# First eight gate/up steps beside the exponentials, their silu made later from DRAM, in a fused S4 and SwiGLU forward and backward kernel

## The chip, the cores and the metric

The kernel runs on one core of a Trainium2 chip. The metric is device microseconds of one execution. Before the change the median of three executions is 1864.86 us (1864.12 to 1871.07); one further execution was taken with the hardware profiler, and its trace is what the views below show.

## The reference, cut to what matters

Tokens L = 2048, channels D = 576, state N = 128, hidden width F = 4608, all in bfloat16. The kernel returns the output and the gradients of all inputs that count, 13 arrays in all.

```python
xn = layernorm(A_u)                                   # [2048, 576]
dt = exp(log_dt)                                      # [576]
K  = Re sum_n C * exp(dt * (A_re + i A_im) * l) * dt * B   # [576, 2048], l = 0..2047
s  = irfft(rfft(xn, 4096) * rfft(K, 4096))[:2048] + xn * Dskip
gate, up = xn @ w1, xn @ w3                           # [2048, 4608] each
g  = silu((silu(gate) * up) @ w2)
out = A_u + s * g
# and the vjp: gradients of A_u, A_re, A_im, B_re, B_im, C_re, C_im, log_dt, Dskip, w1, w3, w2 for grad_out
```

## The kernel before, in words

The program is written on a layer that orders instructions itself: every instruction carries a priority, a time in us set by `pre` (prologue, L145) or `at` (all later stages, L123), and each engine's instruction list is filled by priority as the data dependences allow. On each engine the list is then fixed when the program is built. Three things hold an instruction back beyond its data: `tc.issue_after(x)` puts it behind x; a `Chain` (L62) puts every operation behind the one before it on the same engine; and a generator that yields due times lets one stage weave its steps into another's.

Tokens lie in 16 tiles of 128, channels in five blocks of 128 (the last holds 64). The program's PSUM tiles are of one bank (512 fp32 columns on each partition) or of two, shared out by pools.

**Prologue** (`prologue`, L264 to 372). It loads log_dt, A, B and C (`load_dvec`, `load_dmat`, `load_rates`) and A_u (`ln_load`); A_u's odd token tiles are also kept with their rows turned, in DRAM (`odd_A_u`), and read back from there. It multiplies A_re by dt, splits the product into three bf16 parts (`split3`, L374), stores them (PCS_dram) and loads them back as `lhs_r` with 48 rows. `build_reader` makes SELR, a matrix of selectors. `early_exps` (L498) then forms the real exponents as 108 products of 48 rows by 512 columns, two to a PSUM buffer of two banks (`e_ps`, two buffers), 54 exponentials of 1024 columns by ScalarE (L514), and stores the factors to E_dram. Meanwhile VectorE takes the layer norm's statistics (`ln_stats`; the root by ScalarE's Sqrt), normalises (`ln_normalise`), and TensorE transposes xn to `xnT` (two two-bank buffers `ln_pt`; the 64 channels of the last block are copied to the other half of the partitions by a DMA). GpSimd multiplies C by B (the W products) and builds the selectors SEL. `early_spectra` (L519) makes the DFT of xn, folded by its symmetries, into UH_dram: 32 groups of four products of 288 columns into two two-bank buffers, each copied out by VectorE in one operation of 576 columns.

**Hidden phase** (`ffn_hidden`, L859 to 925). Nine blocks of 512 hidden columns by eight pairs of token tiles make 72 gate/up steps. A step has for each of its two tiles eight products of 512 columns of full depth (L901) and two tail products of depth 64 (L909), into `pg` and `pu` (one bank each, two buffers each). Then ScalarE makes silu into `s_t` (L913), g is copied out by VectorE for the second tile of the pair (L915) and by ScalarE for the first (L917), u by ScalarE (L918). VectorE multiplies h = s * u (L920); SP's queue stores H (L922), GpSimd's queue stores G and U (L924), which the backward pass reads.

**Woven into it** (`ssm_forward`, L469, a generator that `ffn_hidden` draws on by due times): first `ssm_kernel` (L542), 36 chunks of 16 channels that build K from the stored exponentials (load of `E_l` L570, phase products `et_ps` L589, sines `cs_k` by ScalarE L590, products on VectorE L595 to 611, sums over n as 64 matmuls into `kps` L626, copy to `KT` L630); then `ssm_conv` (L788), the convolution in two halves of the channels: DFT of K (`kraw`, L726 to 729), complex products by VectorE (`cmul_acc`, L771), inverse DFT (L761), the sums `ev` and `s_t` (L843 to 846), S to DRAM (L847). Before its chunks `ssm_forward` issues four things for the convolution on SP's queue: the row of Dskip, a turned copy of grad_out's odd tiles (`odd_grad_out`), the DFT matrices to CS_dram and four transposing loads of them (`cT`, `nat_transpose`). By priority all of these land in the prologue's part of the lists.

**Then** the output projection (`ffn_output`, L927, product `po` L976), and the backward pass (from L1034): the convolution's gradients, the parameters' gradients, and three large weight and input gradients.

The call that joins these: the pools of the hidden phase are opened after the prologue's are closed, and `ffn_hidden(wp, gup, fps, 0, 12, ssm_forward(0, 8, 8))` gives steps 6 us apart and chunks and convolution steps 8 us apart in the planner's time.

## Time and profile before

| what | value |
|---|---|
| median of three runs | 1864.86 us |
| profiled execution, time | 1858.3 us |
| its span, first to last instruction | 1856.5 us |
| mean clock granted to TensorE | 0.965 |
| TensorE matmul busy | 1679.0 us, 90% of the span |
| VectorE, ScalarE, GpSimd busy | 1370.5, 909.5 and 354.7 us |
| first product of the exponentials, last exponential done | 35.1 and 122.7 us |
| first gate product | 123.3 us |
| first sine of the chunks, last product of the chunks | 149.3 and 430.1 us |
| last inverse DFT of the convolution | 596.9 us |
| last gate product, first output projection | 598.5 and 598.7 us |

The profile cuts the span in 40 slices of 46 us, with a digit for each engine's busy tenths and one for the clock that TensorE was granted (9 is 90% or more). Its groups give, for a line of the program and an engine, the number of instructions, their busy time and the mean of one. The timeline lists single groups by start. In a table of stretches each engine has its busy time with the number of its instructions in brackets; PEld is TensorE's loading of weights, which lies beside its products. Times count from the span's start.

### The profile page before, as it was taken

The numbers are of one execution on the slowest core, as the hardware profiler recorded it, in microseconds if no ns is written. First come the engines' busy times: TensorE is split into PE (matmuls) and PEld (weight loads), VectorE is DVE, ScalarE is ACT, GpSimd is POOL, SyncE is SP. The second block draws the span as 40 slices with busy tenths as digits, with TensorE's granted clock in tenths as the row PEclk, the third lists the DMA queues.
The fourth block names the chain that finished last, engine by engine and source line by source line (L and its number), as shares of the span: only waits on it lengthen the run. The fifth ranks groups of instructions, "written<-read, shape, count | busy, mean of one in ns | idle before, by whom it ended". The sixth has DMA issues, their size and how long they took to land. (4 is left out here: it accounts for less than half of the span.)

```text
span 1856.5 us, 38320 instructions
## 1 busy us (share of the span) xinstructions
PE 1679.0 (90%) x15461; PEld 1228.5 (66%) x15516; DVE 1370.5 (74%) x2081; ACT 909.5 (49%) x1636; POOL 354.7 (19%) x569
## 2 busy tenths in 40 slices
PE   2899999999897899789999999999999987998997
PEld 0335555555353677678878888888878865786776
DVE  5648766768988455589694888849999954976684
ACT  3768888887563111476665756655544410000101
POOL 4022222222222211011111111111111143131032
PEclk9769999999998999999999999999999998999999
DMA  6579988887777988758666575579999999989994
GB/s 174 189 245 321 334 301 308 307 291 272 229 249 212 240 192 187 231 159 221 178 196 201 164 215 165 173 208 270 254 263 236 203 231 228 233 206 205 202 224 73
DMA packets 627111, 417.13 MB, mean 225 GB/s; under 512 B 425205, under 2 KB 567477, under 8 KB 622325
## 3 DMA queue, kind: packets, MB, share of 16 engines
q1 hardware_dynamic: 568644, 280.65, 60.3%
q0 software_dynamic: 31728, 107.69, 17.2%
q10 hardware_dynamic: 26560, 26.35, 5.0%
q8 instruction: 121, 1.98, 0.4%
q14 instruction: 58, 0.47, 0.1%
HBM read 135.60 MB, written 190.89 MB: 176 GB/s over the span
## 5 line engine op out<-in xcount | busy, mean ns | idle before, releaser
L1672 PEld LDWEIGHTS <-acts 128*128 128x128 bf16 x2304 | 225.8, 99 | 78.2 <-DMA acts<-GG_dram 9.4
L1624 PEld LDWEIGHTS <-xn_bf 128*128 128x128 bf16 x2304 | 224.7, 98 | 34.8 <-issue 8.7
L1241 DVE TENSOR_TENSOR pr_q<-et_ps,pz 128x1024 f32<-128x1024 f32 x144 | 176.0, 1222 | 32.3 <-PE et_ps L1236 24.6
L1672 PE MATMUL px<-wT,acts 128*128 128x288 bf16 x1408 | 181.1, 288 | 4.3 <-DMA wT<-in_B_w_dram 4.3
L901 PEld LDWEIGHTS <-xnT 128*128 128x128 bf16 x1152 | 107.4, 98 | 115.5 <-issue 25.5
L1564 PE MATMUL ph<-w2T,goT 128*128 128x256 bf16 x1440 | 175.3, 277 | 8.6 <-DMA w2T<-w2r 6.8
L1244 DVE TENSOR_REDUCE S_all<-pr_q 128x32 f32<-128x1024 f32 x144 | 175.3, 1217 | 3.3
L901 PE MATMUL pg<-wmB_w,xnT 128*128 128x512 bf16 x526 | 148.1, 383 | 16.1 <-DVE g_t L915 9.5
L1564 PEld LDWEIGHTS <-goT 128*128 128x128 bf16 x1440 | 141.3, 99 | 27.4 <-DMA w2T<-w2r 7.1
L901 PE MATMUL pu<-wmB_w,xnT 128*128 128x512 bf16 x571 | 155.7, 379 | 0.4
L1604 PE MATMUL pgw<-go_o,h_n 128*128 128x288 bf16 x1152 | 150.3, 289 | 6.3 <-DVE h_n L1542 5.5
L1624 PE MATMUL pgw<-gu_n,xn_bf 128*128 128x256 bf16 x1152 | 133.9, 274 | 6.5 <-ACT gw L1608 6.3
L1604 PEld LDWEIGHTS <-h_n 128*128 128x128 bf16 x1152 | 113.3, 99 | 35.2 <-DVE h_n L1542 5.7
L1672 PE MATMUL px<-wA,acts 128*128 128x288 bf16 x896 | 120.4, 292 | 13.8 <-DMA acts<-GG_dram 9.0
L913 ACT ACTIVATE s_t<-pg 128x512 bf16<-128x512 f32 x144 | 87.8, 610 | 89.8 <-PE pu L909 45.1
L1624 PE MATMUL pgw<-gg_n,xn_bf 128*128 128x256 bf16 x1152 | 130.0, 273 | 0.6 <-ACT gw L1626 0.6
L1567 ACT CAST gh<-ph 128x512 bf16<-128x512 f32 x144 | 82.2, 602 | 78.0 <-PE ph L1564 60.5
L590 ACT ACTIVATE cs_k<-et_ps 128x512 bf16<-128x512 int16 x216 | 112.2, 646 | 1.7 <-PE et_ps L589 1.3
L1626 ACT CAST gw<-pgw 128x256 bf16<-128x256 f32 x144 | 53.9, 374 | 95.5 <-PE pgw L1624 90.0
L924 POOL DMA_DIRECT2D G_dram<-g_t x72 | 52.2, 725 | 234.0 <-DVE g_t L915 224.7
L1609 POOL DMA_DIRECT2D out_dram<-gw x36 | 20.0, 555 | 387.1 <-ACT gw L1608 334.1
L918 ACT CAST u_t<-pu 128x512 bf16<-128x512 f32 x144 | 87.1, 605 | 12.3 <-PE pu L901 12.3
(307 smaller groups left out, 3221.5 us busy)
## 6 DMA issues: line engine op xcount, KB each, us to landing
U_dram<-u_t POOLq DMA_DIRECT2D x72, 256.0 KB, 4.3
G_dram<-g_t POOLq DMA_DIRECT2D x72, 256.0 KB, 4.0
H_dram<-h_t SPq DMA_DIRECT2D x72, 256.0 KB, 3.6
Q_dram<-q_k SPq DMA_DIRECT2D x36, 512.0 KB, 4.3
h_n<-U_dram POOLq DMA_DIRECT2D x18, 1024.0 KB, 8.6
gg_n<-G_dram POOLq DMA_DIRECT2D x18, 1024.0 KB, 6.7
GU_dram<-gu_n SPq DMA_DIRECT2D x36, 512.0 KB, 7.8
GG_dram<-gg_n SPq DMA_DIRECT2D x36, 512.0 KB, 9.6
```

Of the source, the lines that this page charges most:

```text
L590: nc.scalar.activation(out=CS[:, :, o:o + 256], in_=pt[:].bitcast(I16)[:, :, 0::2], func=ACT.Sin, scale=6.283184 / 2 ** 16)
L901: ins = nc.tensor.matmul(pt[:], lhsT=xnT[:, c, ts], rhs=wm[w][:, c, :], start=(q == 0 and c == 0), stop=(q == 1 and c == nfull - 1))
L913: nc.scalar.activation(out=s_t[:, :, q, :], in_=pgv, func=ACT.Silu)
L918: nc.scalar.copy(out=u_t[:, :, q, :], in_=pu[:].rearrange("p (g f) -> p g f", g=ng))
L1241: nc.vector.tensor_tensor(out=pr[:].rearrange("p r k e -> p r (k e)"), in0=T[h][:].rearrange("p k z d a -> p (k z d a)")[:, None].to_broad ...
L1244: nc.vector.tensor_reduce(out=self.S_all[:, :, d0:d0 + 4], in_=pr[:].rearrange("p r k (d a) -> p (r k) d a", d=4), op=ALU.add, axis=AX.X)
L1564: self.pe_last = nc.tensor.matmul(ph[j][:, k, :].rearrange("p (a f) -> p a f", f=P), lhsT=lw, rhs=rh, start=(n == 0), stop=(n == nfull))
L1567: self.sc(lambda: nc.scalar.copy(out=gh[:, j], in_=ph[j][:]))
L1604: self.pe_last = nc.tensor.matmul(pgw[pi_][:, 0:pw], lhsT=hn[:, tt, fl * P:(fl + 1) * P], rhs=go_o[:, tt, po:po + pw], start=(tt == 0), st ...
L1624: self.pe_last = nc.tensor.matmul(pw_[:, 0:FG], lhsT=self.xn_bf[:, tt, c * P:(c + 1) * P], rhs=nat[:, tt, :], start=(tt == 0), stop=(tt == ...
L1626: self.sc(lambda: nc.scalar.copy(out=gw[:, c], in_=pw_[:, 0:FG]))
L1672: self.pe_last = nc.tensor.matmul(px[pi_][:, 0:pw], lhsT=acts[i][:, ai, fi, :], rhs=w[:, po:po + pw], start=(n == 0), stop=(n == len(steps ...
```

## The change

**Eight gate steps move into the prologue.** The steps of the first block of hidden columns are issued beside the exponentials, each held behind a given exponential product (the product number 16 + 10 * step). Of these steps VectorE copies out both g and u; silu, product and H store are left out there. The pools of the hidden phase open before the prologue's, and block 0's weights are loaded on SP's queue right behind `lhs_r`. In the first block a step takes two even or two odd tiles, even ones first.

**Their silu comes late.** From step 46 on, behind every third step, `late_silu` loads G and U of one pair of tiles back from DRAM on GpSimd's queue, ScalarE makes silu of 1024 columns, VectorE the product, SP's queue stores H.

**PSUM is cut finer.** The exponentials are made in halves of 512 columns in one-bank buffers, stored after every 1024 columns; transposes of xn and the spectra share two one-bank buffers `t_ps`, a half of 288 columns each, copied out in turn by VectorE and ScalarE. The gate pool's two `pg` and two `pu` are open beside them.

**No elementwise work on GpSimd:** the W products and SEL go to VectorE, the selectors' raw rows are made by GpSimd's iota in bf16 at once. The layer norm's root is made by Newton steps on VectorE in place of ScalarE's Sqrt; statistics and normalising go by even tiles first, odd tiles after. The tail of xnT is written twice by a matmul in place of a DMA.

**Loads by need.** log_dt is loaded as five rows and transposed on TensorE, odd_A_u goes to GpSimd's queue, the other rates are loaded behind `lhs_r`. The convolution's four loads (`conv_loads`) stand in a chain on SP's queue behind the load of `E_l` of chunk 8.

**Pace.** Gate steps 8 to 45 are planned 7 us apart and the rest 5.8 us; `gate_mark` holds a step behind a chunk's phase products or a convolution step's last product; the chunks are 7.2 us apart, the convolution's steps get times of their own, and its buffers `c_s` go from two to three. From step 46 on ScalarE copies all of g; before that VectorE copies it for the second tile, and for the first in every third step.

```diff
@@ ln_stats, ln_normalise
-        self.S.activation(out=sd[:], in_=self.mv[:, :, 1], func=ACT.Sqrt, bias=self.eps_col[:], scale=1.0)
-        self.V.reciprocal(out=self.rstd[:], in_=sd[:])
+    def root(self, small, y, var, n):
...
+        V.tensor_scalar(out=y.bitcast(I32), in0=a[:].bitcast(I32), scalar1=-1.0, scalar2=float(0x5f3759df), op0=ALU.mult,
+                        op1=ALU.add)
+        for _ in range(3):
+            V.scalar_tensor_tensor(out=a[:], in0=y, scalar=-0.5, in1=y, op0=ALU.mult, op1=ALU.mult)
+            V.tensor_tensor(out=a[:], in0=a[:], in1=v[:], op=ALU.mult)
+            V.scalar_tensor_tensor(out=y, in0=a[:], scalar=1.5, in1=y, op0=ALU.add, op1=ALU.mult)
...
@@ prologue
+            nc.scalar.dma_start(out=lr[0:nfull], in_=aps["A_log_dt"][0:nfull * P].rearrange("(c p) -> c p", p=P))
...
+            for k in range(3):
+                self.sy.dma_start(out=LR_[k * 16:(k + 1) * 16], in_=self.PCS_dram[2, k].rearrange("(k p) n -> p k n", p=16))
+            next(gate)
...
+            self.ln_normalise(even, tps, (8, 14))
...
+            self.ln_normalise(odd, tps, (32, 38))
...
-            pl = self.G
+            pl = self.V
...
+            self.exps_last = self.S.prev
+            self.early_spectra(up, tps, 90, 0.3)
+            for n in range(self.EARLY):
+                next(gate)
@@ early_exps
-                pe = ps.tile([P, 1024], FP32, name="e_ps")
+                E = ep.tile([P, 1024], BF16, name="E_k")
                 for k in range(2):
+                    self.pre(17.5 + 0.66 * len(self.exps))
+                    pe = ps.tile([P, 512], FP32, name="e_ps")
...
+                    self.exps.append(self.e_last)
+                    self.S.activation(out=E[:, 512 * k:512 * k + 512], in_=pe[:], func=ACT.Exp)
+                self.e_stores.append(nc.sync.dma_start(out=self.E_dram[c2 // 2, :, o:o + 1024], in_=E[:]))
@@ early_spectra
+                    for ri in range(2):
+                        self.pre(T + TU * (((h * NB + m) * KT + kt) * 2 + ri))
+                        pt = ps.tile([P, 512], FP32, name="t_ps")
...
+                        if ri == 0:
+                            nc.vector.tensor_copy(out=u[:, :, ri, kt, :], in_=src)
+                        else:
+                            with self.tc.issue_after(self.exps_last.ins):
+                                nc.scalar.copy(out=u[:, :, ri, kt, :], in_=src)
@@ ssm_kernel
+                if ch == 8:
+                    self.conv_loads(el)
@@ ffn_hidden
+    def gate_time(self, n):
+        if n < self.EARLY:
+            return -69 + 7.5 * n
+        i = n - self.EARLY
+        return 5 + 7 * i if i < 38 else 271 + 5.8 * (i - 38)
+
+    def gate_mark(self, n):
+        i = n - self.EARLY
+        if i < 38:
+            return 36 * i // 38 - 1
+        h, k = divmod(i - 38, 13)
+        return 36 + 8 * h + (-1, -1, 0, 1, 2, 3, 3, 4, 4, 4, 5, 5, 5)[k]
+
+    def late_silu(self, j, gup):
...
+        for src, dst in ((self.G_dram, g_t), (self.U_dram, u_t)):
+            nc.gpsimd.dma_start(out=dst[:].rearrange("p g t f -> p g (t f)"),
+                                in_=src[0:ng, :, 2 * j:2 * j + 2, :].rearrange("g p t f -> p g (t f)"))
+        nc.scalar.activation(out=s_t[:], in_=g_t[:], func=ACT.Silu)
+        nc.vector.tensor_tensor(out=h_t[:].rearrange("p t (g f) -> p g t f", g=ng), in0=s_t[:], in1=u_t[:], op=ALU.mult)
+        nc.sync.dma_start(out=self.H_dram[2 * j:2 * j + 2, :, 0:ng * FG].rearrange("t p f -> p t f"), in_=h_t[:])
...
+                pair = [4 * (n % 4) + n // 4 + 2 * q for q in range(NT)] if fb == 0 else [NT * n, NT * n + 1]
...
+                                        if early:
+                                            lead = self.exps[16 + 10 * step]
+                                        else:
+                                            lead = self.marks[mark] if mark >= 0 else None
...
-                    if q % 2 == 1:
+                    puv = pu[:].rearrange("p (g f) -> p g f", g=ng)
+                    if early:
                         nc.vector.tensor_copy(out=g_t[:, :, q, :], in_=pgv)
+                        nc.vector.tensor_copy(out=u_t[:, :, q, :], in_=puv)
+                        continue
...
+                    if step >= self.EARLY + 38 or (q == 0 and step % 3):
+                        nc.scalar.copy(out=g_t[:, :, q, :], in_=pgv)
                     else:
-                        nc.scalar.copy(out=g_t[:, :, q, :], in_=pgv)
-                    nc.scalar.copy(out=u_t[:, :, q, :], in_=pu[:].rearrange("p (g f) -> p g f", g=ng))
+                        nc.vector.tensor_copy(out=g_t[:, :, q, :], in_=pgv)
+                    nc.scalar.copy(out=u_t[:, :, q, :], in_=puv)
...
+                late, r = divmod(step - self.EARLY - 38, 3)
+                if late in range(LT // NT) and r == 0:
+                    self.at(T + 3)
+                    self.late_silu(late, gup)
```

More of the change, by code (lines that the diff above doesn't have):

```diff
@@ L77 @@
 class K:
+    EARLY = 8
     def __init__(self, tc, aps: dict, dbg: dict | None = None):
@@ new lines, in ln_stats, with ln_root @@
+            self.V.bn_stats(stats[:, 1, :], self.xs[i][:, half:])
+            if last is not None:
+                self.V.bn_aggr(self.mv[:, last[0], :], last[1][:])
+            last = i, stats
+        return last
+    def ln_root(self, tiles, small, last):
+        self.V.bn_aggr(self.mv[:, last[0], :], last[1][:])
+        sl = slice(tiles[0], tiles[-1] + 1, 2)
+        self.root(small, self.rstd[:, sl], self.mv[:, sl, 1], len(tiles))
+        self.V.scalar_tensor_tensor(out=self.negmr[:, sl], in0=self.mv[:, sl, 0], scalar=-1.0, in1=self.rstd[:, sl],
+                                    op0=ALU.mult, op1=ALU.mult)
@@ L303, in prologue @@
+            nc.tensor.transpose(pd[:].bitcast(BF16)[:, 0:DT], lr[:], self.ident_bf[0:DT, 0:DT])
+            self.S.activation(out=self.dt_col[:], in_=pd[:].bitcast(BF16)[:, 0:DT], func=ACT.Exp)
+            self.dft_angles()
+            self.pre(2)
+            self.selector_rows(st)
+            last = self.ln_stats(even[0:1], small)
             dt_b = self.dt_col[:, :, None].to_broadcast([P, DT, N])
```

450 lines of the change are left out of this document (241 added, 209 removed).

## The prediction

> **What bounds the kernel now.** I read the busy tenths in 40 slices first, then the busy time by stretches that I cut at the program's stages, then the tile view of the exponentials and the order of time inside one stretch.
>
> The slices (46 us each; rows for TensorE and for the clock granted to it):
>
> ```profile
> PE   2899999999897899789999999999999987998997
> ...
> PEclk9769999999998999999999999999999998999999
> ```
>
> TensorE is the fullest engine nearly everywhere; the loss that stands out is slices 1 to 3, where it starts late and then runs at 0.6 to 0.7 of its clock. The stretches are: exponentials alone, exponentials beside the spectra, first gate steps, kernel chunks beside gate steps, convolution beside gate steps, all the rest.
>
> ```profile
> core 0: us, PE busy (x) PEld busy (x) DVE busy (x) ACT busy (x) POOL busy (x), PEclk, DMA share, GB/s
> 35.10:52.00 16.90, 15.39 (x32) 3.96 (x33) 1.03 (x5) 14.64 (x15) 3.37 (x3) 1.00 0.48 186
> 81.30:122.70 41.40, 40.66 (x109) 9.63 (x109) 16.67 (x26) 26.16 (x26) 9.92 (x14) 0.50 0.69 227
> 123.30:149.30 26.00, 25.64 (x139) 12.78 (x141) 17.36 (x31) 13.79 (x25) 4.37 (x6) 0.95 0.75 255
> 149.30:430.40 281.10, 271.76 (x3597) 152.84 (x3633) 199.81 (x276) 243.80 (x484) 68.07 (x94) 1.00 0.88 307
> 430.40:598.70 168.30, 148.37 (x829) 76.23 (x844) 156.99 (x214) 93.89 (x197) 39.59 (x54) 0.96 0.73 239
> 598.70:1856.50 1257.80, 1152.67 (x10631) 960.81 (x10629) 932.84 (x1402) 486.97 (x858) 212.95 (x373) 0.98 0.85 206
> ```
>
> The chunks are bound by TensorE (271.8 of 281.1 us), the convolution by VectorE (157.0 of 168.3). Between 81 and 123 TensorE is busy throughout, but at a clock of 0.50: an exponential (1024 columns) then comes every 1.97 us (21 in 41.4), against 1.06 between 35 and 52. The prologue's start, from the tile view of the exponentials' PSUM:
>
> ```profile
> L514 PE MATMUL e_ps<-SELR,lhs_r x108: 373/606/631, 35.1 to 122.1; 48*128 48x512 bf16 x108
> L72 ACT ACTIVATE E_k<-e_ps x54: 1018/1023/1112, 36.1 to 122.7; 128x1024 bf16<-128x1024 f32 x54
> ...
>   DMA lhs_r<-PCS_dram: 35.1, 1
> ```
>
> The first exponential waits 35.1 us for a chain of loads. And the price of gate work, at the end of the hidden phase, in order of time:
>
> ```profile
> 597.02 1.03 PE L901 MATMUL pg<-wmB_w,xnT 128*128 128x512 bf16 x4
> ...
> 597.88 1.03 PE L901 MATMUL pu<-wmB_w,xnT 128*128 128x512 bf16 x4
> ...
> 598.74 4.08 PE L976 MATMUL po<-w2a,hcA 128*128 128x288 bf16 x32
> ```
>
> Four 512-column matmuls start 0.86 us before the next four: 0.215 us each. A step has 16 of them and two pairs of tails that run together (18 slots): 3.87 us. The output projection starts 0.2 us behind the last gate matmul, so the end of the hidden phase at 598.7 sets everything behind it. From there on the changed program's instruction lists are those of before on all five engines (TensorE's last 21,242 rows are identical), so I keep 1257.8 us for the rest, and the sum is the new time of that end.
>
> **Start of the exponentials.** Logarithmic steps now come as five row descriptors and a transpose, not 576 single elements (landed at 10.6); the swapped rows of A_u go to GpSimd's queue; grad_out's copy (1.15 MB) and the A_im load no longer stand around the loads of lhs_r. A_re was issued at 4.1 and took 4.4 us to land; issued some 2 us earlier it lands near 7. The split into three parts took 4.1 us (11.2 to 15.3), stores 1.9 us to land, so the loads go out at about 13.5. They took 12 us behind 1.15 MB of other data; alone I give them 6.5: first exponential at 20, bounds 17 and 25. ScalarE's sines (3.3 us and two table loads of 1.28) move ahead of it and are done by then; the Sqrt with its two table loads (2.9 us, 52 to 55) is gone, replaced by two chains of 13 tiny VectorE operations (0.15 to 0.19 each, 5 us in all).
>
> **The exponentials, now with eight gate steps.** 108 halves of 512 columns. Counting the changed lists until the last one:
> - TensorE: 108 x 0.215, nine steps x 3.87 (the ninth slips in), 96 transposes at some 0.07, 2.8 for the WT transposes: 68 us at full clock.
> - ScalarE: 108 x 0.53 (half of 1.06), eight WT copies at 0.68: 63 us.
> - VectorE: statistics 15.3, normalising 5.6, xnT copies 7, roots 5, W 8 x 0.82 = 6.6 (on GpSimd 11.1), selectors 2, rates and splits 10.2, folding 5.4, and 32 gate copies x 0.69 = 22.1: 79 us, the fullest, starting near 15.
>
> Three strict orders, linked by two one-bank buffers for the exponentials and two pairs for the gates. An exponential takes between 0.53 us (ScalarE back to back) and 0.98 (half of 1.97, the cold stretch). I take 0.70, nearer the first: the 0.98 belongs to the 0.50 clock, and when gate steps came in at 123 the clock was back at 0.95 over the next 26 us. 108 x 0.70 + 6 for WT = 82: end at 102, bounds 84 and 132. That the eight steps cost no ScalarE time here is the point of copying them out with VectorE.
>
> **Spectra.** In before they ended at 147, half of them beside the exponentials. Now the lists put 60 of the 64 halves behind the last exponential, with only one gate step among them, on two one-bank buffers. One half: two matmuls 0.24, drain 0.16, copy 0.4 (kraw, same 288 columns, 0.41), two hand-overs of 0.1: about 1.0 us per buffer, 0.5 per half: 30 us (37 at half clock). First chunk at 132, with 10.2 steps done (before: 149, with 3.9).
>
> **Chunks.** Before, 716 weight loads of gates in the stretch are 44.75 steps, 173.2 us; the other 98.6 us are the 36 chunks. Now 36.3 steps stand there: 140.5 + 98.6 = 239 us; at the same 3.3% idle 247. ScalarE needs less (a third of a PSUM copy per step goes to VectorE, which has 71% load). The skip_row load, grad_out's copy, the CS store and the cT transposes that stood in SP's queue in the prologue now stand between the E loads of chunks 8 and 9: four transposes (5.9 us of issue) and whatever waits in that order for VectorE. Behind them are H stores and E loads. It is covered by three gate steps; I add 5, bounds 0 and 12. End at 384.
>
> **Convolution.** 25.5 steps are left (before 23.4). VectorE loses all g copies (24 x 0.68 = 16.2) and gains two h products (1.4) and eight late products (8 x 0.68 = 5.4): 147 us busy; with before's 6.7% idle 158. ScalarE: 94 + 26 copies at 0.58 + two steps + eight late silus of 1024 columns (1.02): 123, still off the bound. TensorE: 98.7 + 384 x 0.122 = 146. Two engines near 147, so no better than 150, and no worse than today's 168 unless the late loads block (below). End at 384 + 158 = 542.
>
> **Sum.** 598.7 - 542 = 57 us earlier. The profiled execution (span 1856.5, time 1858.3) would become 1801; it ran 6.6 under the median of the runs (1864.9), so by that median **1808**.
>
> **A rule against it.** The Trainium skill, "TensorE: Matmul & The Clock Gate", section "A second HAM failure mode: psum-queue depth-cycling", says that TensorE which pauses briefly between groups because PSUM buffers turn over can fall back to half clock again and again. Between 81 and 123 this trace shows half clock at 98% busy, which agrees, and speaks against that page's simpler rule (Part 1, "What's actually happening") that a busy window releases the clock. The exponentials' buffers shrink from two banks each to one, so by that rule the pattern would be worse and the time that of the first rival, 1858.
>
> **Rivals.**
> - Cold prologue. For it: the 0.50 row above. Against: 0.95 as soon as dense 128-row gate matmuls joined. TensorE's work at half clock: 46 + 70 + 12 + 3 + 31 for the spectra = 162 us from 20: first chunk at 182, 50 later: 1858, as good as no change.
> - Convolution gains nothing. The late loads and the steps' tiles share three buffers; on GpSimd's queue the next steps' G and U stores stand behind a load that waits for a buffer, and without those stores ScalarE and then TensorE's PSUM wait. For it: GpSimd already waited 79.8 us for u_t there. Against: those waits cost nothing. Eight times 2 us: 174 instead of 158: 1824.
> - Slower: lockstep. Every exponential waits, behind a gate matmul, for one more VectorE copy (0.69): 108 x 0.69 = 75 us, 1883. It decides from 0.70 + 57/108 = 1.23 us per exponential. Against: 32 gate copies for 108 exponentials, a third of that.
> - It doesn't lie beside the exponentials: steps wait for xnT or weights and slip behind. Then 8 x 3.87 = 31 us of the gain goes: 1839.
>
> **Chances.** Forecast 0.60, convolution 0.15, slipped steps 0.08, cold prologue 0.09, lockstep 0.08. The bounds of the terms (start -3/+5, exponentials -18/+30, spectra 0/+7, chunks -5/+7, convolution -8/+10) do not all fall on one side: range 1778 to 1843, which takes in the second and fourth rival. Half a per cent (9.3 us) is about what a measurement of this kernel can tell from no change: faster by more 0.86, within 0.06, slower 0.08.
>
> **What would show it.** First e_ps matmul near 20; last near 102, clock at 0.9 or above between 30 and 100; first cs_k near 132; kps ending near 384 with TensorE above 95% busy; the first po near 542; 1258 us from there to the end. Wrong if the clock stays at 0.5 beside gate steps, if pg matmuls wait for VectorE, if E_l holds VectorE over 10 us, or if the rest changes length.

## The result, and the profile after

The changed kernel takes 1878.86 us in the median of 20 executions (1858.34 to 1903.88); the kernel before, on the same chip, takes 1863.84 us in the median of 20 (1854.77 to 1887.02). The ratio is 1.0059, 95% interval [1.0032, 1.0086]: the change makes the kernel slower, by 0.6%. The forecast was 1808 us with a range of 1778 to 1843, so it missed with its sign as well. Medians here are of all executions, while ratios leave out those that a disturbance lengthened; the first profiled execution of the changed kernel (1903.88 us) was one of these, so the views below are of a second one, named after_again in the experiments (span 1877.7 us, time 1879.51).

The 40 slices of the changed kernel, busy tenths of TensorE and the clock that the throttle's records give it:

```profile
PE   5998989999889799699989999999789977999998
...
PEclk9899989999999899899999999999989988999999
```

The weak slices 1 to 3 of before have filled, and slice 0 holds work. A new hole stands in slices 28 and 29 (1314 to 1408 us), and the one in slice 16 (751 to 798 us) is a tenth deeper. By stages, cut as before: exponentials in two parts, spectra, chunks, convolution, the rest. (125.1 us is the start of the last exponential, which lasts 0.6 us. The 122.7 us of before, called its end there, is also its start; there it lasts 1.0 us.)

```profile
core 0: us, PE busy (x) PEld busy (x) DVE busy (x) ACT busy (x) POOL busy (x), PEclk, DMA share, GB/s
22.30:61.90 39.60, 37.23 (x123) 10.86 (x125) 23.13 (x79) 18.67 (x34) 3.93 (x6) 0.87 0.58 191
61.90:125.10 63.20, 61.65 (x278) 19.80 (x283) 45.54 (x95) 47.88 (x86) 29.46 (x41) 1.00 0.76 244
125.10:157.90 32.80, 24.44 (x144) 13.49 (x144) 16.54 (x35) 17.68 (x43) 2.90 (x4) 1.00 0.76 264
157.90:425.30 267.40, 248.60 (x3457) 144.18 (x3493) 196.18 (x282) 221.13 (x441) 57.11 (x78) 0.97 0.85 295
425.30:593.70 168.40, 150.86 (x854) 75.72 (x865) 147.93 (x198) 111.42 (x233) 53.68 (x73) 0.99 0.82 273
593.70:1877.70 1284.00, 1159.90 (x10631) 965.58 (x10629) 932.07 (x1401) 487.24 (x860) 211.19 (x372) 0.96 0.86 203
```

While the exponentials run, TensorE is busy for 98.9 of 102.8 us and VectorE for 68.7: the engine that the forecast called the fullest is not the bound. In the last row TensorE has the same 10,631 products as before, and the row is 26.2 us longer. Set beside the forecast, whose terms added to a span of 1799.8 us:

| term | forecast, us | after_again, us | difference |
|---|---|---|---|
| first exponential's product | 20 | 22.3 | +2.3 |
| exponentials with gate steps | 82 | 102.8 | +20.8 |
| spectra | 30 | 32.8 | +2.8 |
| chunks | 252 | 267.4 | +15.4 |
| convolution | 158 | 168.4 | +10.4 |
| output projection to end | 1257.8 | 1284.0 | +26.2 |
| sum | 1799.8 | 1877.7 | +77.9 |

The output projection begins at 593.7 us, against 598.7 before: of the 57 us that the hidden phase was to gain, 5 are left, and the rest of the program takes 26 more.

**TensorE in the exponentials.** Its products in order of time, early and a little later in the same execution (start, us, engine, line, names, shape):

```profile
53.44 0.63 PE L1005 MATMUL pg<-wmB_w,xnT 128*128 128x512 bf16 x1
54.01 0.61 PE L556 MATMUL e_ps<-sel_val,lhs_r 48*128 48x512 bf16 x1
54.54 0.61 PE L1005 MATMUL pu<-wmB_w,xnT 128*128 128x512 bf16 x1
...
62.20 0.39 PE L556 MATMUL e_ps<-sel_val,lhs_r 48*128 48x512 bf16 x1
62.52 0.28 PE L219 MATMUL t_ps<-ident_bf,xn_bf 128*128 128x128 bf16 x2
...
64.46 0.61 PE L1005 MATMUL pg<-wmB_w,xnT 128*128 128x512 bf16 x2
65.00 0.39 PE L556 MATMUL e_ps<-sel_val,lhs_r 48*128 48x512 bf16 x1
65.32 0.39 PE L1005 MATMUL pg<-wmB_w,xnT 128*128 128x512 bf16 x1
65.64 0.39 PE L556 MATMUL e_ps<-sel_val,lhs_r 48*128 48x512 bf16 x1
65.96 0.39 PE L1005 MATMUL pg<-wmB_w,xnT 128*128 128x512 bf16 x1
```

Two things are to be seen. Up to about 60 us, apart from 46.6 to 50.0, a lone product of 512 columns takes 0.61 us, from then on 0.39: up to there TensorE runs at half its clock. The clock column says so only in part:

```profile
22.30:46.60 24.30, 23.04 (x86) 7.61 (x88) 16.62 (x57) 11.88 (x21) 0.00 (x0) 1.00 0.70 224
50.00:60.20 10.20, 10.04 (x24) 2.12 (x23) 1.90 (x6) 3.82 (x7) 1.35 (x2) 0.50 0.51 177
```

From 22 to 46 us it reads 1.00 although the products take 0.61 us. The trace's record of the clock has its first entry at 46.6 us, where the clock first rises, and the column counts time ahead of the first entry as full speed; from that entry on, column and durations agree. **Ahead of the first entry, only the duration of a known product tells the clock.** Second, at full clock the starts from 65.00 on lie 0.32 us apart, and the two of the one pg group at 64.46 lie 0.22 apart (0.61 less 0.39): a product that follows one of another row count (48 or 128) starts 0.10 us later than one of the same count. The weight loads show why:

```profile
64.99 0.09 PEld L556 LDWEIGHTS <-lhs_r 48*128 48x128 bf16 x1 [0.42 <-issue]
65.31 0.10 PEld L1005 LDWEIGHTS <-xnT 128*128 128x128 bf16 x1 [0.23 <-issue]
65.63 0.09 PEld L556 LDWEIGHTS <-lhs_r 48*128 48x128 bf16 x1 [0.23 <-issue]
```

Each load of 0.10 us stands directly ahead of its product instead of beside the one before. A product of 64 rows and one of 128 cost the same 0.10 us beside each other, while the five of 48 rows that follow one of 64 at full clock start after 0.21. By the trace, TensorE's list has some 165 changes that cost (48 or 64 rows against 128) up to the last exponential: about 17 us (165 x 0.10), an estimate, that the forecast's list of TensorE work, 68 us, did not have.

### The profile page after: what moved, and what is told of

Read it like the earlier page. It is cut to its first block, busy times and chain, and to the rows that moved or that the text cites. A ratio compares the mean times of both kernels' runs of the same rounds, so it can differ in the third digit from the quotient of the medians.

```text
span 1902.1 us, 38623 instructions
## 1 busy us (share of the span) xinstructions
PE 1706.6 (90%) x15535; PEld 1235.7 (65%) x15535; DVE 1377.8 (72%) x2134; ACT 912.7 (48%) x1698; POOL 365.9 (19%) x592
## 5 line engine op out<-in xcount | busy, mean ns | idle before, releaser
L1744 PEld LDWEIGHTS <-xn_bf 128*128 128x128 bf16 x2304 | 229.5, 100 | 53.1 <-issue 22.6
L1005 PE MATMUL pg<-wmB_w,xnT 128*128 128x512 bf16 x576 | 165.5, 393 | 7.5 <-ACT g_t L1025 7.4
L1005 PE MATMUL pu<-wmB_w,xnT 128*128 128x512 bf16 x576 | 163.1, 391 | 0.1
L1744 PE MATMUL pgw<-gu_n,xn_bf 128*128 128x256 bf16 x1152 | 142.9, 284 | 19.6 <-ACT gw L1728 19.4
L1023 ACT ACTIVATE s_t<-pg 128x512 bf16<-128x512 f32 x128 | 78.2, 611 | 53.1 <-PE pu L1013 25.8
L1037 POOL DMA_DIRECT2D G_dram<-g_t x64 | 46.4, 725 | 273.1 <-DVE g_t L1027 149.6
L1836 ACT ACTIVATE go<-gx 128x576 bf16<-128x576 f32 x16 | 10.9, 683 | 157.1 <-DVE gx L1819 132.9
## 6 DMA issues: line engine op xcount, KB each, us to landing
GG_dram<-gg_n SPq DMA_DIRECT2D x36, 512.0 KB, 11.5
```

The source lines that it names most:

```text
L1005: ins = nc.tensor.matmul(pt[:], lhsT=xnT[:, c, ts], rhs=wm[w][:, c, :], start=(q == 0 and c == 0), stop=(q == 1 and c == nfull - 1))
L1023: nc.scalar.activation(out=s_t[:, :, q, :], in_=pgv, func=ACT.Silu)
L1744: self.pe_last = nc.tensor.matmul(pw_[:, 0:FG], lhsT=self.xn_bf[:, tt, c * P:(c + 1) * P], rhs=nat[:, tt, :], start=(tt == 0), stop=(tt == ...
```

## The experiments

**after_again: no edit.** A second look at the changed kernel.

> The changed kernel once more, unaltered, for a second profile. In the profiled execution of the changed kernel the first chunk's sine came at 160.0, the last kernel product at 427.4, the first output projection at 600.0, and 1302 us followed, where the kernel before has 598.7 and 1257.8. If the hidden phase gained nothing because of its own order of work, the first three come back within 5 us. If the 44 us behind it belong to the change (its buffers lie elsewhere in memory), the rest is again near 1300; if they are a matter of single executions (short stretches of half clock, waits for DMAs), it falls to between 1255 and 1275.

1881.23 us in the median of 4, ratio 1.0105 [1.0045, 1.0166]. It is the profile read above.

**after_rows128: the exponentials' products on 128 rows.** Rows 48 to 127 of lhs_r are zero, so that of the changes of row count only those at the gate steps' tails of 64 rows are left.

```diff
+            nc.gpsimd.memset(LR_[32:64], 0.0); nc.gpsimd.memset(LR_[64:P], 0.0)
-   lhsT=LR_[0:48, c2 + ch, :], rhs=SELR[0:48, o1:o1 + 512]
+   lhsT=LR_[:, c2 + ch, :], rhs=SELR[:, o1:o1 + 512]
```

> The exponentials' products take 128 rows instead of 48 (the added rows of lhs_r are zero); TensorE's order is the same. Theory of row shapes: in the trace of the changed kernel a product behind one of another number of rows starts 0.32 us after it, behind one of the same number 0.215, and its weights are loaded only then; the list has 163 such changes up to the last exponential, of which about 125 lie between 48 and 128 rows: 13 us less, last exponential near 114, first sine near 146, the whole 10 to 17 us faster than the changed kernel. Rival, the PSUM hand-over: two one-bank buffers make ScalarE and TensorE wait for each other, whatever the rows: last exponential at 127, no difference. Second rival, VectorE's gate copies: the same, no difference.

The exponentials take 85.4 us (27.6 to 113.0) instead of 102.8; the first sine comes at 148.1 instead of 157.9. The tail products of the gate steps mark the same places in both lists. From the first exponential's product to the third step's tails it is 33.3 us against 44.0; from there to the ninth step's 45.5 against 53.5. The second stretch runs at full clock in both, so I put its 8.0 us in six steps down to the row changes (109 changes against 17); at that rate the first stretch owes them 4, and the other 6.7 us to the clock: in this run products of 128 rows raise it at 34 us (pairs of products of 1.07 us, then of 0.60), and of the exponentials' time only 41 to 44 us falls back. after_hold (below), whose program is the changed kernel's up to there, bears the split out: its clock is up for good at 45 us instead of 60, its first stretch takes 39.2 us, its second the same 53.5. The forecast's 82 us would have been nearly right without 48 rows. But the whole is 1875.06 us, 1.0081 [1.0036, 1.0126], some 4 us under the changed kernel's median where 10 to 17 were expected: the stages behind take most of the gain back.

**before_rows128: the same edit in the kernel before.**

> The kernel before, with the exponentials' products on 128 rows (zeros in the added ones), otherwise unaltered. Theory: the half clock between 64 and 128 comes from products that use 48 of 128 rows, so that TensorE counts as little used: the clock stays at 1, exponentials come every 1.06 us, the last one near 100, and the whole is 15 to 22 us faster than the kernel before. Rival: it comes from the pauses between products that wait for a PSUM buffer; those stay, and so does the clock of 0.5: no difference.

1854.73 us, 0.9961 [0.9926, 0.9995]: faster, but by half of what was expected. The last exponential starts at 105.7 us instead of 122.7, the output projection begins 14 us earlier, at 584.7, and the rest is 1270.0 us, 12 longer. A pair of the exponentials' products in the kernel before and in this one, in order of time:

```profile
97.74 1.14 PE L533 MATMUL u_ps<-xt,cCS 128*128 128x288 bf16 x4
98.82 1.03 PE L514 MATMUL e_ps<-SELR,lhs_r 48*128 48x512 bf16 x2
99.78 0.66 PE L533 MATMUL u_ps<-xt,cCS 128*128 128x288 bf16 x2
```
```profile
95.76 0.59 PE L514 MATMUL e_ps<-SELR,lhs_r 128*128 128x512 bf16 x2 [0.32 <-ACT E_k L72]
```

With 48 rows a pair lasts 1.03 us, with 128 rows 0.59, and TensorE waits for ScalarE. So the cold prologue (half clock) of the kernel before comes from products of few rows, not from its buffers, which are the same here. Nor does a fuller TensorE explain it: from 40.8 to 52.3 us of this run it is busy 7.4 of 11.5 us and warm (at full clock), while in after_early0, next, it is busy 89% of the time and cold.

**after_early0: no early steps.** All 72 steps stand behind the last exponential, with their silu in place; the other edits of the change stay.

```diff
-    EARLY = 8
+    EARLY = 0
-        return 5 + 7 * i if i < 38 else 271 + 5.8 * (i - 38)
+        return 5 + 5.78 * i if i < 46 else 271 + 5.8 * (i - 46)
```

> All other edits of the change, but no gate step beside the exponentials (the 72 steps all behind the last exponential product, 44 of them in the chunks, no late silu). Theory of row shapes: without gate products between them the exponentials run at ScalarE's pace, 108 x 0.6 + 6 for WT = 71 us from 22: last one near 95 to 100, first sine near 130 with 2.2 steps done, chunks 279, convolution 168: output projection near 577, so 20 us earlier than with the eight steps; the early steps then cost what they bring. Rival: without gate products TensorE's clock falls to half as it did before between 81 and 123 (0.98 us each): last exponential near 135, first sine near 165, output projection near 612.

1897.58 us, 1.0174 [1.0111, 1.0237]. The exponentials run without gate steps, the last one starts at 107.3 us, and the clock is at half to the end. In order of time, and the stretch with its clock column:

```profile
101.59 1.07 PE L556 MATMUL e_ps<-sel_val,lhs_r 48*128 48x512 bf16 x2 [0.19 <-ACT E_k L72]
```
```profile
22.30:107.30 85.00, 75.87 (x229) 20.88 (x230) 51.41 (x141) 63.69 (x116) 9.98 (x14) 1.00 0.66 220
```

The column says 1.00 for 85 us in which pairs take 1.07, because the record's first entry is at 109.8 us. The rival expected the half clock and was right, but not its price: pairs start 1.26 us apart (the next one at 102.85), 0.63 an exponential instead of 0.98. The output projection begins at 607.6 us, so the eight steps with their late silu are worth 14 us against after_again. The chunks take 303 us with 44.4 steps in them, 22 more than the kernel before with 44.7: the other edits cost that. The convolution has 25.4 steps beside it, as many as in after_again, and takes 162.1 us instead of 168.4; here there is no late silu, so by these two profiles it costs some 6 us there. The rest takes 1284.2 us, so a long rest needs neither the early steps nor the late silu.

**after_dram and before_dram: DRAM places exchanged.** The scratch tensors of each stand where the other has them, by seven writes of 8 bytes early on (eight in before_dram).

```diff
+    def place(self):
+        for t in (...):
+            self.nc.sync.dma_start(out=flat[0:4], in_=self.ident_bf[0:1, 0:4])
```

> The changed kernel with its scratch tensors in DRAM at the addresses they have in the kernel before (seven writes of 8 bytes on SP's queue near the start fix the order in which they are placed); the other engines' lists are the same, SP's has only the seven writes more. Three executions of kernels with the change had 1284 to 1302 us behind the first output projection, the kernel before 1258, although the instructions there are the same; 17 to 24 us of it arise between 1300 and 1430 us, where DMA is busy throughout and a transposing load of Q takes 10.4 us to land instead of 5.2. Theory of DRAM places (G and U changed places, Q, PZ and H moved): the rest falls to between 1258 and 1268. Rival, SBUF places or what the hidden phase leaves behind: the rest stays between 1284 and 1302.

> The reverse: the kernel before with its scratch tensors at the changed kernel's addresses in DRAM. Theory of DRAM places: the rest rises from 1258 to between 1275 and 1295, the whole by 17 to 30 us. Rival: no difference, rest between 1256 and 1272 (1270 in the kernel before with exponentials on 128 rows).

1877.41 us, 1.0078 [1.0033, 1.0123], and 1869.55 us, 1.0012 [0.9982, 1.0042]; the rest of after_dram is 1277.7 us, still long. The only profile of before_dram is of its longest execution (1888.3 us, with a rest of 1282.8), so for the reverse the median counts, and it does not rise by the 17 us or more that were expected. The places in DRAM are not the cause.

**after_pad and before_pad: SBUF places.** A constant of four bytes on each partition moves every later tile by 32 bytes, which gives after_pad the places of the kernel before.

```diff
+        self.pad_col = const.tile([P, 1], FP32, name="pad_col")
+        nc.vector.memset(self.pad_col[:], 1e-5)
```

> The changed kernel with a column of four bytes more among its constants, so that the tiles of the backward pass lie at the addresses in SBUF that they have in the kernel before (the change dropped such a column, and all lie 32 bytes lower). Theory of SBUF places: the rest falls from 1284 or more to between 1258 and 1268. Rival, DRAM places: it stays at 1284 to 1302.

> The reverse: the kernel before with such a column more, its later tiles in SBUF 32 bytes higher. If places in SBUF count, the rest changes by 15 us or more; by the theory of DRAM places it stays at 1256 to 1272. It is also one more profile of the kernel before.

1886.41 us, 1.0059 [1.0015, 1.0103], with 1286.8 for the rest; and 1861.23 us, 0.998 [0.9952, 1.0007], with 1255.2. Not the cause either.

**after_wA and before_wA: an earlier load.** Five pairs of transposing loads of w1 and w3 (`wA`) go from groups 11 to 15 of the weight gradients to groups 4 to 8.

```diff
-                    if stage == "end" and 0 <= gi - GP < cfg.DT:
+                    if stage == "end" and 0 <= gi - 4 < cfg.DT:
```

> The changed kernel with the ten transposing loads of w1 and w3 into wA moved seven groups ahead, from the stretch where DMA is busy throughout (1270 to 1450 us) to one where it is busy 0.72 (1000 to 1200); TensorE's, VectorE's, ScalarE's and GpSimd's lists are the same. In all seven traces with the change one pair of these loads took 15 to 24 us instead of 8, beside the 1 MB load of gg_n, while DMA moved 35 to 100 GB/s; in the kernel before only one trace of four has it. Theory: this collision is 17 to 24 us of the rest; without it the rest is 1262 to 1270, the whole about 18 us faster than the changed kernel. Rival: DMA is full there anyway and other loads collide (qT, w2T): the rest stays at 1278 or more.

> The same move in the kernel before, which had the collision in one trace of four: the rest stays at 1255 to 1262, the median falls by the quarter that had it, 3 to 6 us. If it falls by 15 us or more, the stretch was worth that in the kernel before too, and the collision does not separate the two kernels.

1881.83 us, 1.0116 [1.0071, 1.016], and 1873.61 us, 1.0079 [1.0054, 1.0104]. Neither gains. Both now lose 11 to 12 us between 1240 and 1276 us of the kernel before's time, where TensorE waits 8.6 and 10.0 us for a load of `gz`.

before_wA shows the clock column once more. Its stretch of the exponentials, to be held against the row 81.30 to 122.70 of the kernel before in the prediction:

```profile
81.30:122.00 40.70, 38.94 (x104) 9.21 (x103) 16.78 (x27) 27.63 (x31) 9.92 (x14) 1.00 0.65 208
```

The column reads 1.00 where it read 0.50, with much the same busy share and the last exponential at 125.9 instead of 122.7 us; its pairs take 1.03 us like those of the kernel before. Here the record's first entry is at 128.2 us, in the kernel before at 60.9.

**after_conv_spread: the convolution's loads apart.** The chain behind chunk 8 is issued one by one, behind the E loads of chunks 8 and 10 to 20.

```diff
-                if ch == 8:
-                    self.conv_loads(el)
+                if 8 <= ch < 22 and ch % 2 == 0:
+                    self.conv_load((ch - 8) // 2, el)
```

> The changed kernel with the seven issues for the convolution on SP's queue one by one behind the E loads of chunks 8, 10, ... 20, in place of all behind chunk 8. In the traces with the change SP issues nothing between 209 and 225 us, the next two E loads leave at 233, the sines wait 5.8 us for VectorE, TensorE 6.2 us for the sines, and the clock is at half for 13 us behind it (6.8 us lost). Theory: 10 to 13 us less in the chunks (last kernel product near 413 instead of 425 to 427). Rival: the stall comes from something else in the order of chunk 8 and stays: no difference.

What it was to mend, in after_again: SP's queue in order of time, a wait from 205 to 258 us (engine, line, releaser: us, times, longest), and a stretch with its busy times and clock.

```profile
208.62 0.46 SPq L72 DMA_DIRECT2D CS_dram<-cCS  x1
225.39 0.34 SPq L650 DMA_DIRECT2D PZ_dram<-p_k  x1
225.78 0.42 SPq L655 DMA_DIRECT2D Q_dram<-q_k  x1
226.30 6.34 SPq L72 DMA_TRANSPOSE cT<-CS_dram  x4
232.68 0.58 SPq L1034 DMA_DIRECT2D H_dram<-h_t  x1
233.32 0.46 SPq L618 DMA_DIRECT2D E_l<-E_dram  x1
```
```profile
PE et_ps L639 <- ACT cs_k L641: 7.7, 3, 6.2
```
```profile
232.00:252.00 20.00, 13.16 (x160) 6.71 (x159) 13.53 (x20) 7.32 (x15) 2.18 (x3) 0.66 0.85 276
```

SP's queue issues nothing for 16 us, because the next store waits for a chunk's product `p_k`; then come four transposing loads, and the next chunk's E load only at 233.3. TensorE has nothing but gate steps in the meantime, waits up to 6.2 us for a sine, and from 232 to 252 us is busy 13.2 of 20 us at a recorded clock of 0.66. Of those 20 us, 6.8 are idle; and from 237.7 to 251.4 us the clock is at half with TensorE busy for 11.05 us, of which half, 5.5 us, is lost: some 12 of the chunks' 15.4 us, by this estimate. But with the loads spread the hole moved to 296 to 352 us, around chunk 20: chunks 265.4 instead of 267.4 us where 10 to 13 us less were expected, the whole 1876.9 us, 1.0082 [1.005, 1.0114]. Where the four loads stand makes only 2 us.

**after_all: the mends together.** 128 rows, spread loads, earlier wA, and G of the late silu loaded two steps ahead into a buffer of its own (and `c_s` back to two buffers).

```diff
+                if late in range(LT // NT) and r == 0:
+                    self.late_load(late, self.latep)
-                if late in range(LT // NT) and r == 0:
+                if late in range(LT // NT) and r == 2:
                     self.late_silu(late, gup)
```

> The changed kernel with four edits: exponentials on 128 rows, convolution loads spread, wA loads moved, and G of the late silu loaded two steps ahead into a buffer of its own (ScalarE waited 17.6 us for these loads; c_s has two buffers again to make room). If the costs are separate, they add up: chunks from 147 (10 to 12 us earlier), last kernel product near 402, output projection near 565, rest 1262 to 1270: about 1830, 2% faster than the kernel before. If they hide one another (the output projection's first epilogue waits for loads that stand behind the last H stores whatever comes before), between 1845 and 1860.

1875.38 us, 1.008 [1.005, 1.011]; both expectations, 1830 and 1845 to 1860, were missed. The output projection begins at 584.2 us, 10 earlier than in after_again, and the rest takes 1287.2. The convolution, by its waits in after_again and then here:

```profile
ACT s_t L940 <- DMA g_t<-G_dram: 13.3, 5, 3.6
...
DVE h_t L1032 <- ACT u_t L1028: 8.7, 5, 5.3
```
```profile
DVE h_t L1040 <- DMA H_dram<-h_t: 11.7, 2, 11.5
...
ACT s_t L1031 <- DMA S_dram<-s_t: 9.5, 1, 9.5
```

ScalarE's waits for G are gone, but stores of H and S that leave late now hold VectorE and ScalarE: 166.6 us instead of 168.4.

**after_hold, before_hold, before_rows128_hold: two kinds of load kept apart.** In after_again a pair of wA loads held SP's queue for 18.6 us beside a 1 MB load `gg_n`; in the kernel before the pairs held it for 4.2 to 8.2. Here gg_n waits for the pair.

```diff
+            a, b = (part[3][0:1, 0, do:do + 4] for part in self.wT_[0:2])
+            self.gp(lambda: nc.gpsimd.tensor_tensor(out=gg[0:1, 0, 0:4], in0=a, in1=b, op=ALU.add))
         self.gp(lambda: nc.gpsimd.dma_start(out=gg[:], in_=self.G_dram[gi]))
```

> The changed kernel, but in groups 13 to 17 of the backward pass the 1 MB load gg_n of the next group waits until the wA pair of transposing loads, which in the changed kernel's trace it meets, has landed (a sum of four elements of the two, written by GpSimd into the tile that the load then overwrites). Theory collision (two kinds of load beside each other make the DMA slow, a pair takes 15 to 24 us in place of 8): each wA pair lands within 10 us, the stretch 1250 to 1450 loses some 13 us or more, from the output projection to the end 1265 us or less, median 1862 to 1868. Rival, the DMA is full there whoever meets whom: gg_n comes later by what the pair gains, ScalarE's first silu of a group waits for it, rest 1273 to 1290, median 1875 to 1890.

> The same wait in the kernel before, where the pair took 7 to 8 us in four of five groups. Theory collision: nothing to gain, rest 1255 to 1262 us, ratio 0.998 to 1.003. Rival, full DMA: the load that is held comes late in the group, rest 1262 to 1275, ratio 1.003 to 1.010.

> The kernel before with the exponentials' products on 128 rows and this wait; without the wait it had 1854.7 us, 0.9961 [0.9926, 0.9995], and 1270.0 us from the output projection to the end, 12 more than before. Theory collision: the rest falls to some 1258 and the median to 1843 to 1850 (0.988 to 0.993). Rival, full DMA: 1853 to 1860, no gain over the version without the wait.

1879.17 us, 1.0047 [1.0008, 1.0086]; 1877.16 us, 1.004 [1.0007, 1.0074]; 1863.2 us, 0.9984 [0.9955, 1.0013]. The pairs now hold the queue for 2.9 to 5.9 us (7.9 once), and nothing is gained: between 1276 and 1465 us of the kernel before's time, where after_again falls back 21 us against it, these fall back 12, 20 and 14. The stretch in the kernel before and in after_again (the last three columns are clock, DMA share and GB/s; the share is of packet times and passes 1 here):

```profile
1276.00:1465.00 189.00, 179.26 (x1753) 154.98 (x1751) 183.69 (x196) 96.99 (x156) 22.98 (x39) 0.99 1.05 248
1276.00:1465.00 189.00, 163.32 (x1538) 139.95 (x1537) 164.02 (x174) 83.73 (x135) 21.32 (x36) 0.94 1.04 226
```

What the engines wait for there, from 1285 to 1475 us, in after_again and then in after_hold:

```profile
PE et_ps L1356 <- DMA gz<-gK_dram: 17.3, 4, 10.4
PEld L1356 <- issue: 16.4, 7, 10.6
```
```profile
POOL gg_n L1651 <- DMA wA<-in_B_w_dram: 25.5, 3, 9.3
...
ACT L1663 <- DMA gg_n<-G_dram: 14.5, 5, 5.7
```

The late `gz` behind the slow pair is gone, and a late gg_n is there in its place. The theory that the meeting of these two loads is the price has fallen by the medians; its rival, that the DMA is full there in any order, fits the shares of 1.05 and 1.04 but is not shown to be the cause, since the kernel before runs through the same full stretch 21 us faster. Note that after_hold's profiled execution (1861.23 us, with a rest of 1265.4) is the fastest of its twelve; up to the output projection it runs the changed program, with its clock up for good at 45 us instead of 60 and its first sine 5 us earlier.

**after_silu_copy: the late silu left out.** A copy from DRAM to DRAM puts u where H should stand.

```diff
-                    self.late_silu(late, gup)
+                    for t in (2 * late, 2 * late + 1):
+                        nc.gpsimd.dma_start(out=self.H_dram[t, :, 0:FB].rearrange("p (g f) -> g p f", g=ng), in_=self.U_dram[0:ng, :, t, :])
```

> The changed kernel without the late silu: in place of its loads, silu, product and store a copy from DRAM to DRAM puts u of the first block's pairs where H should stand, so the first block's hidden activations lack the factor silu(g). This prices the late silu in the convolution and at the start of the output projection. Theory (ScalarE's 17.6 us of waits for g_t hold TensorE's PSUM, and the last products h_t with their waits delay the projection's first epilogues): convolution 158 to 162 us instead of 168, and the 10 us between the first and third sgo gone, median 1858 to 1866. Rival (VectorE and the DMA bind it anyway): convolution 165 or more, median 1873 or more.

1912.49 us, 1.0207 [1.0142, 1.0271]; the kernel leaves out the first block's factor silu(g). It cannot price the late silu: without it the planner wove ScalarE's, GpSimd's and SP's lists anew, also ahead of the copies (chunks 290.4 us, convolution 178.7), so that more than the late silu differs. One part of the theory is seen in its profile: the loss of some 10 us at the first epilogues of the output projection, described below, is gone, as in after_early0.

## Why the prediction was wrong, point by point

- **Start of the exponentials: right** within its bounds (22.3 us; forecast 20, bounds 17 and 25). In four of the other profiles with the change it was 26.3 to 28.8, beyond them, two of these with the prologue unaltered.
- **Exponentials, 82 us: mis-sized, and its list of TensorE work was the step that failed.** "68 us at full clock" left out the row changes (8.0 us measured in six steps, about 17 by count) and some 35 us at half clock (6.7 us by the run on 128 rows). "TensorE's work at half clock" stood as the rival, set aside with the words that 0.95 came "as soon as dense 128-row gate matmuls joined". Beside the exponentials it did not: the clock rose for good only at 60 us, behind two gate steps. And 0.98 us per exponential was put down to the 0.50 clock because the row 35.10:52.00 shows 1.00 at half that pace; but the record of the kernel before has its first entry at 60.9 us, and the 34 products up to 52.5 us took 0.58 to 0.63 us each, so they were cold too, at 0.53 us per exponential. What the stretch from 81 us had besides was the spectra's products on a cold TensorE. 128 rows brought 85.4 us.
- **The rule against it** named the right symptom with another cause. The Trainium skill, "TensorE: Matmul & The Clock Gate", section "A second HAM failure mode: psum-queue depth-cycling", puts it on buffers that turn over; in before_rows128 the same buffers with 128 rows ran at 0.59 a pair, and a TensorE busy for 98% of its time, which the prediction took to agree, leaves little room for pauses. Its section "Seeing it yourself" warns that the recorded clock events are unreliable; here they agree with the durations wherever they exist, and what misleads is the time ahead of the first one (before_wA: up to 128.2 us).
- **Spectra: right** (32.8 for 30).
- **Chunks, 252 us: mechanism right, size wrong.** The steps moved out as counted. The stall at the convolution's loads was named with 5 us and a bound of 12; it cost some 12, by the estimate above, because TensorE's list has only gate steps in the 25 us in which no E load leaves SP's queue. Spreading the loads moved the stall and gained 2 us, so what sets it is only in part shown.
- **Convolution, 158 us: wrong.** The rival "convolution gains nothing" came true in size (168.4, as today) and only partly by its mechanism: ScalarE waits for late G, but without those waits late stores take their place. VectorE lost the work as counted (147.9 us busy for 147), and it was not the bound. By after_early0 the late silu costs some 6 us there; what sets the other 162 is open.
- **"I keep 1257.8 us for the rest": the step that cost most, 26 us.** The forecast gave this term no range because the lists are the same; equal instruction lists did not make equal times here. Some 6 of the 26 us can be the draw of two executions (the profile of before ran 5.5 us under its median, after_again 0.7 over), which leaves about 20 to the change. In nine profiles with the change (all but the first one and after_silu_copy's) the rest took 1265 to 1293 us, in six without it (all but before_dram's) 1255 to 1278. The loss sits in two places. From the first epilogue of the output projection to the third, six of the nine lose 10 to 12 us. In after_again VectorE there waits for a store of H and then twice for S, and TensorE for VectorE to free its PSUM:

```profile
598.27 0.69 DVE L1032 TENSOR_TENSOR h_t<-s_t,u_t 128x1024 bf16<-128x1024 bf16 x1 [6.85 <-DMA H_dram<-h_t]
616.42 0.76 DVE L1110 TENSOR_TENSOR gos<-go_t,s_t 128x576 f32<-128x576 bf16 x1 [17.46 <-DMA s_t<-S_dram]
621.73 0.76 DVE L1110 TENSOR_TENSOR gos<-go_t,s_t 128x576 f32<-128x576 bf16 x1 [4.54 <-DMA s_t<-S_dram]
624.63 5.20 PE L1096 MATMUL po<-w2a,hcC 128*128 128x288 bf16 x21 [13.14 <-DVE e L1108]
```

  In after_hold, the same program up to there, the first wait for S is 10.7 us, the second 0.2, TensorE waits 3.3 us as in the kernel before, and nothing is lost: GpSimd issued the loads of S 5 us earlier there (601.9 instead of 607.1 us) and they landed sooner. So this is chance in part; after_early0, without late silu, has no loss either. The second place is 1200 to 1465 us of the kernel before's time, with 10 to 29 us in each of the nine. Places in memory, the wA loads' position and their meeting with gg_n are excluded as its cause. The kernel before is not safe from it: before_dram's profile loses 21 us there too. **Why the changed program always arrives there in an order that loses, and the kernel before mostly does not, stays open**; that an earlier end of the hidden phase need not reach the end of the whole is seen in single profiles (after_all: 10 us earlier, rest 3 us longer; before_rows128: 14 earlier, rest 12 longer, and a median 7.5 us lower).
- **The rivals.** "Cold prologue" came in part: half clock up to 60 us, for 6.7 us instead of 50. "Slower: lockstep" named the right sign with the wrong mechanism: between the first exponential's product and the last, TensorE's waits for PSUM are 2.3 us, for ScalarE, and none for VectorE. "It doesn't lie beside the exponentials" was wrong: nine steps were done when the last exponential was.

The best version is before_rows128, one edit that the change does not contain: 0.9961 [0.9926, 0.9995].

## What to carry to other kernels

Before work is moved beside other work on TensorE, count the places where its products change their row count, and read its clock from the duration of a known product wherever the clock's record has no entry yet. A stage whose DMA is busy throughout is not a constant: leave a range for it even when its instruction list is identical, and test an early gain by the time of the end. When a stage hidden behind loads is shortened, ask first whether the loads allow an earlier end.

## What the runs showed of the hardware that was not expected

- Products of 48 rows did not raise TensorE's clock: 85 us of them at 1.07 a pair in after_early0, with TensorE busy 89% of the time. With 128 rows, five eighths of them zeros in one operand, a pair took 0.59 from 4 us behind the first product on in before_rows128, and 0.60 from 6 us on in after_rows128. The Trainium skill, "TensorE: Matmul & The Clock Gate", section "What's actually happening", gives the warm-up as a time of some 3.4 us and not a number of matmuls; the 128-row runs fit that, the 48-row run does not.
- A change of row count between 128 and 48 or 64 costs 0.10 us (starts 0.32 us apart instead of 0.22), and the weight load no longer lies beside the product before. From 64 to 48 rows it cost nothing (0.21).
- The trace's record of the clock begins with the first rise (46.6 us in after_again, 60.9 in the kernel before, 109.8 in after_early0, 128.2 in before_wA). Ahead of it the clock column reads 1.00 though products of 512 columns take 0.61 us; behind it the two agree.
- Over the 20 executions of the changed kernel the time goes with the mean recorded clock (correlation -0.96, some 34 us for each 0.01); over those of the kernel before it does not (16 runs: 0.01; 29 runs: -0.39). That fits a record that takes in the cold stretch in some executions and not in others, at the same pace, as in the two traces above (first entry at 60.9 and at 128.2 us).
